# Moving sums, products and bit blocks to other slots in a hash-attention and gated-MLP kernel

## The chip, the cores and the metric

The kernel runs on one core of a Trainium2 chip. The metric is the device time of one execution in microseconds (us). A core has a matrix engine (TensorE, "PE" in the profile; its weight loads are "PEld"), VectorE (DVE), ScalarE (ACT), GpSimd (POOL), and SyncE (SP), which here only issues DMAs. Each engine works through its own list of instructions in order; an instruction that waits holds up everything behind it on that engine.

## The reference

There are 4 batches of 8 heads, 768 tokens and a head size of 64. Each query and key gets a 6-bit bucket from the signs of a projection; attention is allowed only where the buckets agree. The result is 3072 tokens of 512 features, which go through a gated MLP with a residual.

```python
q_bits = (np.einsum('bhsd,dk->bhsk', q, proj) > 0)      # k likewise; 6 bits make a bucket
mask = q_bucket[:, :, :, None] == k_bucket[:, :, None, :]
scores = np.where(mask, scale * q @ k.T, -1e9)
x = softmax(scores) @ v                                  # (3072, 512) after the heads are joined
ffn_out = (gelu(x @ w_gate) * (x @ w_val)) @ w_out       # d_ff = 1536
out = x + sigmoid(x @ w_res) * ffn_out
```

## The kernel before

**Blocks, pairs and slots.** A batch is a block, and has four pairs of heads, so pairs 0 to 15 in all. A pair's scores are made in 9 chunks of 1024 columns (two heads, 71 contracted rows: 64 of the head, 6 bits, one constant). One chunk is a slot, so block b has 36 slots. "Slot 2.5" below is slot 5 of block 2; in the code it is `('a', 2, 5)`. In each slot TensorE computes the scores of its chunk into one of two PSUM tiles `sp` (L500), ScalarE takes the exponential of it (L511), and TensorE multiplies the exponentials of two slots earlier with the values (L475) into an accumulator `av`, one for each head, two buffers.

**Accumulators.** From pair 4 on, an accumulator is opened two slots ahead by a VectorE memset (`opened`, L442), gets a first matmul from TensorE (`preset`, L450), is copied over by VectorE (`repeat`, L454), and when it is full VectorE divides it into the tokens `x_tok` (`finish`, L419 and L420). These slots are fixed by the loop at L606.

**The MLP of the block before** runs in the same slots: `project` (L557 for the residual gate, L571 for the output, one PSUM tile `fps`) hands TensorE two or three matmuls a slot; ScalarE makes `th` (L561), VectorE evicts `fps` with two instructions (L574, L577), SyncE stores.

**Gate and value.** After the 36 slots of a block come twelve steps in `gate_val`, m = 0 to 11; "step g1.9" below is m = 9 of block 1, `('g', 1, 9)` in the code. Each has 8 matmuls for the gate, a gelu by ScalarE into a tile `gt` (L542), 8 matmuls for the value, and a product of the two by VectorE into `hh` (L545). What is listed for a step is issued behind that product. The first step needs the block's tokens turned: a DMA (L428) moves `x_tok` into `x_sb` once the last `finish` of the block is done.

**Bits.** The queries and keys of later pairs get their bits in one of two ways. Pairs 8, 9, 12 and 13 (and 4 to 7 earlier) are transposed by VectorE (L273), hashed on TensorE (L284), and VectorE writes the bits in blocks of four small instructions (`bits`, L305). Pairs 10, 11, 14 and 15 are done without TensorE: for each of the four tensors of two pairs, 12 times, GpSimd multiplies half of the tensor with one column of the projection (`product`, L335, tile `pr`), VectorE sums over the 64 features (`add_up`, L341), and at the end GpSimd compares the sums with zero (`bits_sums`, L344) and SyncE turns the finished rows with a DMA (`turn`, L360). In the text a product and its sum have the same number, 0 to 47 in each block; the products of pair 10 and 11 are block 1's, those of pair 14 and 15 are block 2's. The lists `PLACES`, `LAYS`, `LDY` and `DRAIN` say where each product, each comparison with its turn, each load and the last sums stand.

**What orders the sums.** A product that is put somewhere also puts one sum there, ahead of it, as soon as two products are outstanding; the sum taken is always the oldest product that has none. Products in slots write to the tiles of tag `gt`, shared with gelu's outputs; products in steps write to those of tag `th`, shared with ScalarE's `th`. Each tag has two buffers (L140), so a product waits until the sum of the product two before it in that tag is done. Where the tag changes, the sums left over go to the next block's slot 0, or to the block's slot 35. Block 2's products begin while the last of block 1 are being made, and both use the `gt` buffers in turn.

**Values.** GpSimd also prepares the values of each pair (`vals_s`, `vals_a`, L386 to L398), eight slots ahead of the pair, and casts queries and keys to bf16 (L263, L265).

```python
            if len(left) > 1:
                left.pop(0)
                put(where, b, i, add_up)
            y, n = work[k]
            put(where, b, i, lambda y=y, n=n, tag=tag: product(y, n, tag))
```

Of the kernel before, what the change touches and what calls it, by code (L numbers as in the profile page):

```python
# [80 lines left out]
    (2, 'bits', 4, 0, 'v'), (2, 'turn_dma', 4, 0), (2, 'bits', 4, 1, 'v'), (2, 'turn_dma', 4, 1),  # L81
    (3, 'bits', 5, 0, 'v'), (3, 'turn_dma', 5, 0), (4, 'bits', 5, 1, 'v'), (4, 'turn_dma', 5, 1),
    (1, 'tokens', (6, 7), True), (4, 'cast', 6, 0, 'p'), (5, 'cast', 6, 1, 'p'), (7, 'cast', 7, 0, 'p'),
    (6, 'cast', 7, 1, 'p'), (7, 'bits', 6, 0, 'v'), (7, 'turn_dma', 6, 0), (10, 'bits', 6, 1, 'v'),
    (10, 'turn_dma', 6, 1), (9, 'bits', 7, 0, 'v'), (9, 'turn_dma', 7, 0), (10, 'bits', 7, 1, 'v'),
    (10, 'turn_dma', 7, 1),
]
XDMA = 2
# [4 lines left out]
def kernel(  # L93
# [28 lines left out]


    LDX, TRX, CSX = 9, 26, 26
    LDY = {1: [('a', 1, 0), ('a', 1, 0), ('a', 1, 3), ('a', 1, 1)], 2: [('a', 2, 0), ('a', 2, 2), ('a', 2, 19), ('a', 2, 19)]}
    CSY = [(5, 's'), (5, 's'), (10, 's'), (10, 's')]
    PLACES = {1: [('a', 1, 9), ('a', 1, 10), ('a', 1, 10), ('a', 1, 11), ('a', 1, 13), ('a', 1, 15), ('a', 1, 15), ('a', 1, 16), ('a', 1, 17), ('a', 1, 18), ('a', 1, 18), ('a', 1, 21), ('a', 1, 22), ('a', 1, 23), ('a', 1, 24), ('a', 1, 26), ('a', 1, 27), ('a', 1, 30), ('a', 1, 34), ('g', 1, 0), ('g', 1, 0), ('g', 1, 0), ('g', 1, 1), ('g', 1, 2), ('g', 1, 3), ('g', 1, 3), ('g', 1, 4), ('g', 1, 5), ('g', 1, 5), ('g', 1, 6), ('g', 1, 6), ('g', 1, 7), ('g', 1, 7), ('g', 1, 8), ('g', 1, 8), ('g', 1, 9), ('g', 1, 9), ('g', 1, 10), ('g', 1, 10), ('g', 1, 11), ('a', 2, 2), ('a', 2, 3), ('a', 2, 5), ('a', 2, 6), ('a', 2, 8), ('a', 2, 9), ('a', 2, 13), ('a', 2, 14)], 2: [('a', 2, 1), ('a', 2, 2), ('a', 2, 13), ('a', 2, 14), ('a', 2, 16), ('a', 2, 18), ('a', 2, 19), ('a', 2, 23), ('a', 2, 24), ('a', 2, 24), ('a', 2, 26), ('a', 2, 31), ('a', 2, 32), ('a', 2, 33), ('g', 2, 0), ('g', 2, 0), ('g', 2, 0), ('g', 2, 0), ('g', 2, 1), ('g', 2, 2), ('g', 2, 3), ('g', 2, 3), ('g', 2, 4), ('g', 2, 5), ('g', 2, 5), ('g', 2, 6), ('g', 2, 6), ('g', 2, 7), ('g', 2, 8), ('g', 2, 8), ('g', 2, 9), ('g', 2, 9), ('g', 2, 10), ('g', 2, 10), ('a', 3, 0), ('a', 3, 4), ('a', 3, 4), ('a', 3, 4), ('a', 3, 6), ('a', 3, 7), ('a', 3, 8), ('a', 3, 13), ('a', 3, 13), ('a', 3, 14), ('a', 3, 14), ('a', 3, 15), ('a', 3, 15), ('a', 3, 16)]}
    DRAIN = {1: ('a', 2, 16), 2: ('a', 3, 20)}
    LAYS = {1: [('g', 1, 7), ('g', 1, 8), ('a', 2, 5), ('a', 2, 17)], 2: [('g', 2, 7), ('g', 2, 8), ('a', 3, 6), ('a', 3, 21)]}
    PRS = (1, 8)  # L130
    NE = 9
    C = 2048.0
# [25 lines left out]
    def load(p, side, eng=None):  # L158
        b, hp = divmod(p, HP)
        s = ld_pool.tile([P, HT, D], FP32, tag=f"ld{side}", name=f"ld{side}")  # L160
        (eng or nc.sync).dma_start(
            s.rearrange("p (h t) d -> p h (t d)", h=2),
            (q, k)[side][b, 2 * hp:2 * hp + 2].rearrange("h (p t) d -> p h (t d)", t=T))
        raw[p, side] = s
# [90 lines left out]
    def cast(p, side, eng, c0=0, c1=HT):  # L255
        x = (p, side)
        scale = (1.0 / C) if side == 0 else 1.0
        sl = slice(c0, c1)
        dst = nat_of(x)[:, sl, 0:D]
        if eng is nc.scalar:  # L260
            nc.scalar.activation(dst, raw[x][:, sl], AF.Copy, scale=scale)
        elif side == 0:
            eng.tensor_scalar(dst, raw[x][:, sl], scale, 1.0, op0=ALU.mult, op1=ALU.mult)  # L263
        else:
            eng.tensor_copy(dst, raw[x][:, sl])  # L265
# [325 lines left out]
    def at(s, *pieces):  # L591
        side_work.setdefault(s, []).extend(pieces)
# [4 lines left out]
    def gv(b, m, *pieces):  # L597
        gv_work.setdefault((b, m), []).extend(pieces)
# [23 lines left out]
    def lay(b, m, x):  # L622
        gv(b, m, lambda: bits(*x), lambda: turn(*x))

    def put(where, b, i, *pieces):
        if where == "g":
            gv(b, i, *pieces)
        else:
            at(b * NSLOT + i, *pieces)

    def spread_out(ys, places, drain, lays):
        work = [(y, n) for y in ys for n in range(2 * NBITS)]
        assert len(places) == len(work)
        left, tagged = [], None
        for k, (where, b, i) in enumerate(places):
            tag = "th" if where == "g" else "gt"
            if tagged not in (None, tag):
                for _ in left:
                    put("a", b, 0 if tag == "gt" else NSLOT - 1, add_up)
                left = []  # L640
            tagged = tag
# [5 lines that stand above are left out]
            left.append((y, n))  # L647
        for _ in left:
            put(*drain, add_up)
        for y, p in zip(ys, lays):  # L650
            put(*p, lambda y=y: bits_sums(y), lambda y=y: turn(*y))

    for b in range(B - 1):
# [10 lines left out]
        for m, x in zip((0, 1, 2, 4), xs):  # L664
            lay(b, m, x)
        for y, (where, bb, i) in zip(ys, LDY[b]):
            put(where, bb, i, lambda y=y: load(y[0], y[1]))
        for y, (m, eng) in zip(ys, CSY):
            gv(b, m, lambda y=y, eng=eng: cast(*y, ENG[eng]))
        spread_out(ys, PLACES[b], DRAIN[b], LAYS[b])  # L670
    at(NSLOT + PRS[0], load_rows)
# [31 lines left out]
    def first_gv(i):  # L703
# [8 lines left out]
        cast=lambda p, side, e, *c: cast(p, side, ENG[e], *c),  # L712
# [4 lines left out]
        turn_dma=turn,  # L717
# [14 lines left out]
    for s in range(NSLOT, LAST):  # L732
        p, c = divmod(s, NCH)
# [60 lines left out]
```

## Time and profile before

| | |
|---|---|
| median of three runs | 339.64 us (339.56 to 339.67) |
| the profiled execution | 339.34 us, of which 337.3 us are the span of the trace |
| TensorE busy | 332.4 us of the span |
| VectorE, ScalarE, GpSimd busy | 216.3, 213.8, 175.0 us |
| slots of block 1 | from 78.7 to 120 us of the span |
| slots of block 2 | from 157.4 to 199 us |
| slots of block 3 | from 235.9 to 277 us |

All times within the trace are counted from the span's start. A row of the timeline gives the start, the time until the last of the merged instructions ends, the engine, the line, the operation, the tiles, the shape, the count, and in brackets how long the engine had been idle and what ended that. The recorded ends of matmuls overlap their successors, so waits of TensorE are read from the distance between starts.

### The profile page before, as it was taken

The numbers are of one execution on the slowest core, as the hardware profiler recorded it, in microseconds if no ns is written. First come the engines' busy times: TensorE is split into PE (matmuls) and PEld (weight loads), VectorE is DVE, ScalarE is ACT, GpSimd is POOL, SyncE is SP. The second block draws the span as 40 slices with busy tenths as digits, with TensorE's granted clock in tenths as the row PEclk, the third lists the DMA queues.
The fourth block names the chain that finished last, engine by engine and source line by source line (L and its number), as shares of the span: only waits on it lengthen the run. The fifth ranks groups of instructions, "written<-read, shape, count | busy, mean of one in ns | idle before, by whom it ended". The sixth has DMA issues, their size and how long they took to land.

```text
span 337.3 us, 7740 instructions
## 1 busy us (share of the span) xinstructions
PE 332.4 (99%) x3086; PEld 204.0 (60%) x3086; DVE 216.3 (64%) x458; ACT 213.8 (63%) x247; POOL 175.0 (52%) x260
## 2 busy tenths in 40 slices
PE   8999999999999999999999999999999999999996
PEld 7767665565666655565666665665566665666444
DVE  7977575554577958876577896876577444343243
ACT  4889962337999952437999982255999984322220
POOL 4779920235299943578799972567879100000000
PEclk9999999999999999999999999999999999999999
DMA  7998999999965223518068933825050340000012
GB/s 228 370 289 125 217 242 202 179 166 205 313 222 149 72 85 81 109 32 187 3 167 229 273 92 94 134 47 96 1 126 33 80 101 33 31 2 0 31 64 94
DMA packets 74387, 43.88 MB, mean 130 GB/s; under 512 B 52544, under 2 KB 71360, under 8 KB 74352
## 3 DMA queue, kind: packets, MB, share of 16 engines
q1 hardware_dynamic: 67872, 37.95, 45.3%
q0 software_dynamic: 6400, 5.44, 10.7%
q8 instruction: 24, 0.39, 0.5%
q14 instruction: 11, 0.09, 0.1%
q10 hardware_dynamic: 80, 0.00, 0.0%
HBM read 29.56 MB, written 6.29 MB: 106 GB/s over the span
## 4 chain that ended last, share of the span: by engine, by line
PE 83%; POOL 8%; ACT 4%; DVE 3%; issue 1%; DMA 1%; POOLq 0%; DVEq 0%; ACTq 0%
PE sp L525 37%; PE fps L571 14%; PE sp L500 14%; PE av L475 7%; PE rps L557 5%; POOL pr L335 4%; PE hs L284 3%; ACT ering L511 3%; ACT e L511 1%; PE wps L229 1%; PE pt L373 1%; POOL v L394 1%; DMA x_sb<-x_tok 1%; DVE sums L341 1%; POOL va L386 1%
## 5 line engine op out<-in xcount | busy, mean ns | idle before, releaser
L511 ACT ACTIVATE e<-sp 128x1024 bf16<-128x1024 f32 x117 | 117.7, 1027 | 8.6 <-PE sp L500 3.7
L335 POOL TENSOR_TENSOR pr<-ld,projr 128x384 f32<-128x384 f32 x96 | 93.8, 998 | 47.0 <-DVE sums L341 31.9
L542 ACT ACTIVATE gt<-sp 128x768 bf16<-128x768 f32 x48 | 38.9, 810 | 83.7 <-PE sp L525 80.0
L500 PE MATMUL sp<-aug,aug 71*128 71x256 bf16 (+1 forms) x384 | 86.0, 325 | 0.5
L571 PE MATMUL fps<-wo,hh 128*128 128x512 bf16 (+2 forms) x312 | 79.6, 362 | 0.0
L545 DVE TENSOR_TENSOR hh<-gt,sp 128x768 bf16<-128x768 bf16 x48 | 45.8, 954 | 42.9 <-PE sp L525 39.5
L525 PE MATMUL sp<-x_sb,wg 128*128 128x512 bf16 (+1 forms) x384 | 70.9, 326 | 0.0
L525 PE MATMUL sp<-x_sb,wv 128*128 128x512 bf16 (+1 forms) x384 | 70.9, 326 | 0.0
L475 PEld LDWEIGHTS <-e 128*128 128x128 bf16 x936 | 43.5, 97 | 25.9
L341 DVE TENSOR_REDUCE sums<-pr 128x6 f32<-128x384 f32 x96 | 50.2, 542 | 10.8 <-POOL pr L335 10.3
L525 PEld LDWEIGHTS <-wg 128*128 128x128 bf16 x384 | 37.1, 98 | 25.8 <-issue 1.5
L525 PEld LDWEIGHTS <-wv 128*128 128x128 bf16 x384 | 37.5, 98 | 24.9 <-issue 0.2
L475 PE MATMUL av<-va,e 128*128 128x65 bf16 x936 | 47.0, 193 | 0.0
L571 PEld LDWEIGHTS <-hh 128*128 128x128 bf16 x312 | 28.1, 97 | 21.6
L500 PEld LDWEIGHTS <-aug 71*128 71x128 bf16 x384 | 29.2, 97 | 11.6 <-issue 2.7
L574 DVE SCALAR_TENSOR_TENSOR fps<-th,fps 128x512 f32<-128x512 f32 (+2 forms) x26 | 17.0, 653 | 25.9 <-PE fps L571 25.8
L557 PE MATMUL rps<-wr,x_sb 128*128 128x512 bf16 x96 | 27.1, 379 | 0.0
L511 ACT ACTIVATE ering<-sp 128x1024 bf16<-128x1024 f32 x27 | 25.8, 1031 | 1.7 <-PE sp L500 1.4
L561 ACT ACTIVATE th<-rps 128x512 f32<-128x512 f32 x24 | 14.3, 594 | 18.7 <-PE rps L557 17.5
L273 DVE STREAM_TRANSPOSE t<-ld 128x768 f32<-128x768 f32 (+3 forms) x28 | 23.1, 843 | 1.7 <-DMA ld<-in_q_dram 1.0
L454 DVE COPY av<-av 128x390 f32<-128x390 f32 x24 | 13.6, 565 | 14.6 <-PE av L450 14.5
L263 POOL TENSOR_SCALAR nat<-ld 128x768 bf16<-128x768 f32 (+1 forms) x12 | 9.6, 804 | 19.3 <-DMA aug<-nat 17.4
(76 smaller groups left out, 257.4 us busy)
## 6 DMA issues: line engine op xcount, KB each, us to landing
ldv<-in_v_dram SPq DMA_DIRECT2D x16, 384.0 KB, 5.8
out_dram<-o SPq DMA_DIRECT2D x23, 256.0 KB, 2.3
ld<-in_q_dram SPq DMA_DIRECT2D x15, 384.0 KB, 5.6
ld<-in_k_dram SPq DMA_DIRECT2D x15, 384.0 KB, 5.8
wg<-in_moe_w_gate_dram POOLq DMA_DIRECT2D x4, 384.0 KB, 9.9
wv<-in_moe_w_val_dram POOLq DMA_DIRECT2D x4, 384.0 KB, 10.7
wo<-in_moe_w_out_dram POOLq DMA_DIRECT2D x3, 512.0 KB, 7.6
wr<-in_moe_w_res_dram POOLq DMA_DIRECT2D x1, 512.0 KB, 16.6
```

The lines of the kernel that those rows point to most:

```text
L273: nc.vector.transpose(t32[p, side][:, sl].rearrange("p c h n -> p (c h n)"), raw[p, side][:, sl].rearrange("p c d -> p (c d)"))
L335: nc.gpsimd.tensor_mul(pr, raw[x][:, hi * T:(hi + 1) * T], projr[:, bit].unsqueeze(1).to_broadcast([P, T, D]))
L341: nc.vector.reduce_sum(sums[x][:, hi * T:(hi + 1) * T, bit], pr, axis=mybir.AxisListType.X)
L475: nc.tensor.matmul(av[p, hi][:, qt, :], e[:, off:off + P], va[:, hi, jt, 0:D + 1], start=first, stop=(repeats(p, hi) and jt == T - 1), ski ...
L500: nc.tensor.matmul(sp[:, off:off + nq * P], ks[0:KA, hi * T + jt, :], qs[0:KA, hi * T + qt0:hi * T + qt0 + nq, :], start=True, stop=True)
L511: nc.scalar.activation(e, sp, AF.Exp, scale=float(ALPHA))
L525: nc.tensor.matmul(sp[:, c0:c1], w[:, kk, bass.ts(m, P)], xs[:, kk, c0:c1], start=(kk == 0), stop=(kk == KM - 1))
L542: nc.scalar.activation(gt, sp[:, 0:S], AF.Gelu)
L545: nc.vector.tensor_mul(hidden[b][:, m, :], gt, ps[1][:, 0:S])
L557: nc.tensor.matmul(rps, x_sb[b][:, kk, t, :], wr[:, kk, :], start=(kk == 0), stop=(kk == KM - 1))
L571: nc.tensor.matmul(fps[:, cs], hh[:, m, bass.ts(t, P)], wo[:, m, cs], start=(m == 0), stop=(m == KF - 1))
L574: nc.vector.scalar_tensor_tensor(fps[:, cs], th[:, cs], 1.0, fps[:, cs], op0=ALU.add, op1=ALU.mult)
```

## The change

Nothing is added and nothing is taken away: the same instructions are issued, some of them at other places of their engine's list.

- Block 0, steps: two blocks of bits (four VectorE instructions each) stand one step earlier, pair 7's queries at g0.8 and pair 6's keys at g0.9. Their turns stay.
- Block 1, loads: two loads of pair 11 stand in slot 1.2, one of pair 14 in slot 2.3.
- Block 1, slots 9 to 18 and 29: products 1 and 2 stand in slot 1.9, one slot earlier; products 5 and 17 one slot earlier; products 6 and 7 one slot later; the sums go with them.
- Block 1, steps 9 to 11, and block 2's first slots: products 35 to 39 leave the steps and stand in slot 2.0, with the sums of 33 to 37; they now use the `gt` buffers. Products 40 to 47 stand up to two slots earlier. Two comparisons with their turns (pair 10) stand at g1.8 and g1.11, that of pair 11's keys one slot later.
- Block 2's products: two in block 2 one slot earlier; comparisons of pair 14's queries one step later; in block 3 products 34, 35 and 38, 41 and 45 to 47 one or two slots up or down, the last two sums one slot earlier, two comparisons one slot up or down.

Because `opened`, `repeat` and `finish` stay in their slots, a moved sum can now stand on the other side of one of these memsets or copies on VectorE.

```diff
-    (6, 'cast', 7, 1, 'p'), (7, 'bits', 6, 0, 'v'), (7, 'turn_dma', 6, 0), (10, 'bits', 6, 1, 'v'),
-    (10, 'turn_dma', 6, 1), (9, 'bits', 7, 0, 'v'), (9, 'turn_dma', 7, 0), (10, 'bits', 7, 1, 'v'),
+    (6, 'cast', 7, 1, 'p'), (7, 'bits', 6, 0, 'v'), (7, 'turn_dma', 6, 0), (9, 'bits', 6, 1, 'v'),
+    (10, 'turn_dma', 6, 1), (8, 'bits', 7, 0, 'v'), (9, 'turn_dma', 7, 0), (10, 'bits', 7, 1, 'v'),
...
-    LDY = {1: [('a', 1, 0), ('a', 1, 0), ('a', 1, 3), ('a', 1, 1)], 2: [('a', 2, 0), ('a', 2, 2), ('a', 2, 19), ('a', 2, 19)]}
+    LDY = {1: [('a', 1, 0), ('a', 1, 0), ('a', 1, 2), ('a', 1, 2)], 2: [('a', 2, 0), ('a', 2, 3), ('a', 2, 19), ('a', 2, 19)]}
...
     PLACES = {1:
-      ('a', 1, 9), ('a', 1, 10), ('a', 1, 10), ('a', 1, 11), ('a', 1, 13), ('a', 1, 15), ('a', 1, 15), ('a', 1, 16), ('a', 1, 17),
+      ('a', 1, 9), ('a', 1, 9), ('a', 1, 9), ('a', 1, 11), ('a', 1, 13), ('a', 1, 14), ('a', 1, 16), ('a', 1, 17), ('a', 1, 17),
...
-      ('a', 1, 30), ('a', 1, 34),
+      ('a', 1, 29), ('a', 1, 34),
...
-      ('g', 1, 9), ('g', 1, 9), ('g', 1, 10), ('g', 1, 10), ('g', 1, 11), ('a', 2, 2), ('a', 2, 3),
-      ('a', 2, 5), ('a', 2, 6), ('a', 2, 8), ('a', 2, 9), ('a', 2, 13), ('a', 2, 14)
+      ('a', 2, 0), ('a', 2, 0), ('a', 2, 0), ('a', 2, 0), ('a', 2, 0), ('a', 2, 1), ('a', 2, 2),
+      ('a', 2, 3), ('a', 2, 5), ('a', 2, 8), ('a', 2, 8), ('a', 2, 11), ('a', 2, 13)
     2:
-      ('a', 2, 13), ('a', 2, 14)  ...  ('a', 2, 26), ('a', 2, 31)
+      ('a', 2, 12), ('a', 2, 14)  ...  ('a', 2, 25), ('a', 2, 31)
...
-      ('a', 3, 0), ('a', 3, 4), ('a', 3, 4), ('a', 3, 4), ('a', 3, 6), ('a', 3, 7), ('a', 3, 8),
-      ('a', 3, 13), ('a', 3, 13), ('a', 3, 14), ('a', 3, 14), ('a', 3, 15), ('a', 3, 15), ('a', 3, 16)
+      ('a', 3, 1), ('a', 3, 3), ('a', 3, 4), ('a', 3, 4), ('a', 3, 5), ('a', 3, 7), ('a', 3, 8),
+      ('a', 3, 12), ('a', 3, 13), ('a', 3, 14), ('a', 3, 14), ('a', 3, 17), ('a', 3, 17), ('a', 3, 18)
-    DRAIN = {1: ('a', 2, 16), 2: ('a', 3, 20)}
-    LAYS = {1: [('g', 1, 7), ('g', 1, 8), ('a', 2, 5), ('a', 2, 17)], 2: [('g', 2, 7), ('g', 2, 8), ('a', 3, 6), ('a', 3, 21)]}
+    DRAIN = {1: ('a', 2, 17), 2: ('a', 3, 19)}
+    LAYS = {1: [('g', 1, 8), ('g', 1, 11), ('a', 2, 5), ('a', 2, 18)], 2: [('g', 2, 8), ('g', 2, 8), ('a', 3, 7), ('a', 3, 20)]}
```

More of the change, by code (lines that the diff above doesn't have):

```diff
@@ L124 @@
     LDX, TRX, CSX = 9, 26, 26
-    LDY = {1: [('a', 1, 0), ('a', 1, 0), ('a', 1, 3), ('a', 1, 1)], 2: [('a', 2, 0), ('a', 2, 2), ('a', 2, 19), ('a', 2, 19)]}
+    LDY = {1: [('a', 1, 0), ('a', 1, 0), ('a', 1, 2), ('a', 1, 2)], 2: [('a', 2, 0), ('a', 2, 3), ('a', 2, 19), ('a', 2, 19)]}
     CSY = [(5, 's'), (5, 's'), (10, 's'), (10, 's')]
-    PLACES = {1: [('a', 1, 9), ('a', 1, 10), ('a', 1, 10), ('a', 1, 11), ('a', 1, 13), ('a', 1, 15), ('a', 1, 15), ('a', 1, 16), ('a', 1, 17), ('a', 1, 18), ('a', 1, 18), ('a', 1, 21), ('a', 1, 22), ('a', 1, 23), ('a', 1, 24), ('a', 1, 26), ('a', 1, 27), ('a', 1, 30), ('a', 1, 34), ('g', 1, 0), ('g', 1, 0), ('g', 1, 0), ('g', 1, 1), ('g', 1, 2), ('g', 1, 3), ('g', 1, 3), ('g', 1, 4), ('g', 1, 5), ('g', 1, 5), ('g', 1, 6), ('g', 1, 6), ('g', 1, 7), ('g', 1, 7), ('g', 1, 8), ('g', 1, 8), ('g', 1, 9), ('g', 1, 9), ('g', 1, 10), ('g', 1, 10), ('g', 1, 11), ('a', 2, 2), ('a', 2, 3), ('a', 2, 5), ('a', 2, 6), ('a', 2, 8), ('a', 2, 9), ('a', 2, 13), ('a', 2, 14)], 2: [('a', 2, 1), ('a', 2, 2), ('a', 2, 13), ('a', 2, 14), ('a', 2, 16), ('a', 2, 18), ('a', 2, 19), ('a', 2, 23), ('a', 2, 24), ('a', 2, 24), ('a', 2, 26), ('a', 2, 31), ('a', 2, 32), ('a', 2, 33), ('g', 2, 0), ('g', 2, 0), ('g', 2, 0), ('g', 2, 0), ('g', 2, 1), ('g', 2, 2), ('g', 2, 3), ('g', 2, 3), ('g', 2, 4), ('g', 2, 5), ('g', 2, 5), ('g', 2, 6), ('g', 2, 6), ('g', 2, 7), ('g', 2, 8), ('g', 2, 8), ('g', 2, 9), ('g', 2, 9), ('g', 2, 10), ('g', 2, 10), ('a', 3, 0), ('a', 3, 4), ('a', 3, 4), ('a', 3, 4), ('a', 3, 6), ('a', 3, 7), ('a', 3, 8), ('a', 3, 13), ('a', 3, 13), ('a', 3, 14), ('a', 3, 14), ('a', 3, 15), ('a', 3, 15), ('a', 3, 16)]}
@@ L128 @@
-    DRAIN = {1: ('a', 2, 16), 2: ('a', 3, 20)}
-    LAYS = {1: [('g', 1, 7), ('g', 1, 8), ('a', 2, 5), ('a', 2, 17)], 2: [('g', 2, 7), ('g', 2, 8), ('a', 3, 6), ('a', 3, 21)]}
+    PLACES = {1: [('a', 1, 9), ('a', 1, 9), ('a', 1, 9), ('a', 1, 11), ('a', 1, 13), ('a', 1, 14), ('a', 1, 16), ('a', 1, 17), ('a', 1, 17), ('a', 1, 18), ('a', 1, 18), ('a', 1, 21), ('a', 1, 22), ('a', 1, 23), ('a', 1, 24), ('a', 1, 26), ('a', 1, 27), ('a', 1, 29), ('a', 1, 34), ('g', 1, 0), ('g', 1, 0), ('g', 1, 0), ('g', 1, 1), ('g', 1, 2), ('g', 1, 3), ('g', 1, 3), ('g', 1, 4), ('g', 1, 5), ('g', 1, 5), ('g', 1, 6), ('g', 1, 6), ('g', 1, 7), ('g', 1, 7), ('g', 1, 8), ('g', 1, 8), ('a', 2, 0), ('a', 2, 0), ('a', 2, 0), ('a', 2, 0), ('a', 2, 0), ('a', 2, 1), ('a', 2, 2), ('a', 2, 3), ('a', 2, 5), ('a', 2, 8), ('a', 2, 8), ('a', 2, 11), ('a', 2, 13)], 2: [('a', 2, 1), ('a', 2, 2), ('a', 2, 12), ('a', 2, 14), ('a', 2, 16), ('a', 2, 18), ('a', 2, 19), ('a', 2, 23), ('a', 2, 24), ('a', 2, 24), ('a', 2, 25), ('a', 2, 31), ('a', 2, 32), ('a', 2, 33), ('g', 2, 0), ('g', 2, 0), ('g', 2, 0), ('g', 2, 0), ('g', 2, 1), ('g', 2, 2), ('g', 2, 3), ('g', 2, 3), ('g', 2, 4), ('g', 2, 5), ('g', 2, 5), ('g', 2, 6), ('g', 2, 6), ('g', 2, 7), ('g', 2, 8), ('g', 2, 8), ('g', 2, 9), ('g', 2, 9), ('g', 2, 10), ('g', 2, 10), ('a', 3, 1), ('a', 3, 3), ('a', 3, 4), ('a', 3, 4), ('a', 3, 5), ('a', 3, 7), ('a', 3, 8), ('a', 3, 12), ('a', 3, 13), ('a', 3, 14), ('a', 3, 14), ('a', 3, 17), ('a', 3, 17), ('a', 3, 18)]}
```

## The prediction

> **What bounds the kernel now.** I read the page first, then the chain of waits, then the timeline of TensorE beside those of the engines that release it.
>
> ```profile
> span 337.3 us, 7740 instructions
> PE 332.4 (99%) x3086; PEld 204.0 (60%) x3086; DVE 216.3 (64%) x458; ACT 213.8 (63%) x247; POOL 175.0 (52%) x260
> PE 83%; POOL 8%; ACT 4%; DVE 3%; issue 1%; DMA 1%; POOLq 0%; DVEq 0%; ACTq 0%
> ```
>
> ```profile
> 123.78 2.73 DMA x_sb<-x_tok
> 314.15 2.59 PE fps L571 x12
> ```
>
> TensorE is the bound: busy for 99% and 83% of the chain. Twelve full matmuls follow each other in 2.59 us, so one takes 0.216, and a greater distance between two starts is a wait. Going along TensorE's starts this way I find six waits of 0.05 or more after 78 us. One, behind a gelu of ScalarE in block 3, is not touched; the change can win no more than the sum of the other five. The 8% of POOL in the chain are spells in which TensorE was released just in time; they tell where TensorE would be caught if GpSimd were later.
>
> **The change, place by place.** No instruction is added or dropped, so each part costs only by order. The durations are one profiled execution's, 339.34 us (337.3 of span and 2.04 around it), 0.30 under the median of 339.64; I take the gain off the median unscaled.
>
> *Place 1, the bits at g0.8 and g0.9.*
>
> ```profile
> 77.34 2.01 DVE L305 TENSOR_SCALAR nat<-htp 32x72 bf16<-32x72 f32 x8
> 79.38 0.95 DVE L545 TENSOR_TENSOR hh<-gt,sp 128x768 bf16<-128x768 bf16 x1
> 79.98 0.38 PE L571 MATMUL fps<-wo,hh 128*128 128x512 bf16 x1
> 80.39 0.59 PE L500 MATMUL sp<-aug,aug 71*128 71x256 bf16 x3
> ```
>
> TensorE could go on at 79.98 + 0.216 = 80.20 and went on at 80.39, when the last gate product had freed its `sp`: 0.19 lost. That product stood behind eight bit instructions in 2.01 us. Four of them now stand two steps back, where VectorE is idle, so they cost nothing; the queue before the last product ends 1.0 earlier, and the product starts when its inputs are there, some 0.4 earlier, and ends about 79.9. Gain 0.19. What is late next is TensorE's own work. SyncE's turns wait for the same bits and get no later.
>
> *Place 2, products 1 to 8 of block 1.*
>
> ```profile
> 93.07 0.99 POOL L335 TENSOR_TENSOR pr<-ld,projr 128x384 f32<-128x384 f32 x1 [3.62 <-DVE sums L341]
> 96.89 7.71 POOL L335 TENSOR_TENSOR pr<-ld,projr 128x384 f32<-128x384 f32 x8
> 108.45 0.55 DVE L341 TENSOR_REDUCE sums<-pr 128x6 f32<-128x384 f32 x1 [1.71 <-POOL pr L335]
> 110.17 0.11 DVE L442 MEMSET av<- 128x65 f32 x1
> 109.86 0.60 PE L500 MATMUL sp<-aug,aug 71*128 71x512 bf16 x2
> 110.34 0.20 PE L450 MATMUL av<-vsum,eps_sb 128*128 128x65 bf16 x1
> ```
>
> The accumulator's memset at 110.17 stands behind a sum that waited 1.71 for its product; TensorE's `preset` came at 110.34, where 109.86 + 0.216 + 0.216 leaves 110.29: 0.05 lost. GpSimd had waited 3.62 for the first sum. That sum now stands one slot earlier, so GpSimd resumes about 2 us earlier; the next sums give back some of that (6 and 7 stand a slot later), and I carry 1 us. The memset then comes at about 109.1. Gain 0.05. At the other end, if nothing of the lead survives, it is 0.
>
> *Place 3, the turn of block 1's tokens (product 17 at 1.29).*
>
> ```profile
> 121.18 0.55 DVE L341 TENSOR_REDUCE sums<-pr 128x6 f32<-128x384 f32 x1 [0.39 <-POOL pr L335]
> 121.65 0.69 DVE L574 SCALAR_TENSOR_TENSOR fps<-th,fps 128x512 f32<-128x512 f32 x1
> 123.20 0.56 DVE L420 TENSOR_TENSOR x_tok<-av,rec 128x384 bf16<-128x384 f32 x1
> 123.76 2.75 PE L571 MATMUL fps<-wo,hh 128*128 128x512 bf16 x12
> 126.56 0.48 PE L525 MATMUL sp<-x_sb,wg 128*128 128x512 bf16 x2
> ```
>
> TensorE was done with the twelve matmuls at 123.76 + 2.59 = 126.35 and got the turned tokens at 126.56: 0.21 lost. The chain behind it is the last product, the last sum (121.18), two evictions, `finish`, and a DMA of 2.73. Of the 1 us of lead some 0.8 reaches the last sum. TensorE itself comes 0.24 earlier by places 1 and 2, so 0.45 of lead is enough. Gain 0.21, between 0 and 0.21. Moving product 17 in front of a transpose costs nothing: GpSimd's list there keeps its total.
>
> *Place 4, products 35 to 39 in slot 2.0.*
>
> ```profile
> 157.62 0.95 DVE L545 TENSOR_TENSOR hh<-gt,sp 128x768 bf16<-128x768 bf16 x1 [0.72 <-PE sp L525]
> 158.49 1.01 DVE L341 TENSOR_REDUCE sums<-pr 128x6 f32<-128x384 f32 x2
> 159.59 0.60 ACT L561 ACTIVATE th<-rps 128x512 f32<-128x512 f32 x1 [0.20 <-DVE sums L341]
> 160.09 3.89 ACT L511 ACTIVATE e<-sp 128x1024 bf16<-128x1024 f32 x4
> 160.60 0.41 PE L475 MATMUL av<-va,e 128*128 128x65 bf16 x8
> 161.16 0.59 PE L500 MATMUL sp<-aug,aug 71*128 71x512 bf16 x2
> 163.81 0.19 PE L450 MATMUL av<-vsum,eps_sb 128*128 128x65 bf16 x1
> ```
>
> ScalarE's `th` shares its tile with the products of the steps and waited until 159.50 for sum 38. The next exponential followed it, and TensorE waited for that at 161.16 (eight small matmuls from 160.60 end about 160.85): 0.31 lost. With the change the last product in that tag is 34, so `th` waits for sum 33, the first behind 157.62: 0.46 earlier. The wait goes, 0.31 won at this spot.
>
> It comes back in two ways. First, products 37 to 39 now need sums that come only behind the last gate product: 33, 34, 35 end at 158.49 + 1.01 + 0.46 = 159.96, product 37 starts at 160.03, 39 ends two spacings of 7.71/8 = 0.96 and one duration of 0.99 later at 162.94, its sum at 163.56, and only then comes the memset of slot 2.3, done at 163.69. `preset` follows at 163.74, against 163.81 before. Won there is 0.07, not 0.31. Second, GpSimd is full to the end of the block:
>
> ```profile
> 159.12 1.96 POOL L335 TENSOR_TENSOR pr<-ld,projr 128x384 f32<-128x384 f32 x2 [0.65 <-DMA ld<-in_q_dram]
> 165.15 1.00 POOL L335 TENSOR_TENSOR pr<-ld,projr 128x384 f32<-128x384 f32 x1 [0.25 <-DVE sums L341]
> 168.10 1.95 POOL L335 TENSOR_TENSOR pr<-ld,projr 128x384 f32<-128x384 f32 x2 [1.95 <-DVE sums L341]
> 172.00 1.95 POOL L335 TENSOR_TENSOR pr<-ld,projr 128x384 f32<-128x384 f32 x2 [0.56 <-DVE sums L341]
> 173.91 1.00 POOL L394 TENSOR_TENSOR v<-ldv 128x384 f32<-128x384 f32 x1
> 176.78 4.82 POOL L335 TENSOR_TENSOR pr<-ld,projr 128x384 f32<-128x384 f32 x5
> ```
>
> ```profile
> 172.00:199.63 27.63, 27.63 (x322) 17.31 (x320) 22.15 (x47) 25.41 (x28) 27.10 (x39) 1.00 0.87 230
> ```
>
> ```profile
> 202.27 1.21 SPq L428 DMA_TRANSPOSE x_sb<-x_tok  x1
> 205.08 0.38 PE L525 MATMUL sp<-x_sb,wg 128*128 128x512 bf16 x1
> ```
>
> From 172.00 GpSimd is busy 27.10 of 27.63 (the fifth engine's figure in this row of the windows), up to the last product, whose sum holds the turn of block 2's tokens: issued at 202.27, landed 2.73 later at 205.00, used at 205.08. There is no slack. Between 159.12 and the values at 173.91 GpSimd idled 0.25 + 1.95 + 0.56 = 2.76. Now it starts this stretch 0.91 later (160.03) with two products more (1.92), 2.83 in all, against at most 2.76 of idle time to be filled. Walking its new list I find every sum just done in time, so the idle time is filled and the values come 0.07 later. The turn lands at 205.07, TensorE goes on about 205.11. The whole stage from 157 to 205 then brings -0.03, not +0.31. Bounds: +0.31 if GpSimd should be 0.3 earlier than I count, -2.8 if its idle time stays.
>
> The moved comparisons delay turns that have time: pair 11's first is some 1.5 later, and SyncE's store and loads behind it too, which are needed several slots on. Loads moved by a slot cost nothing for the same reason.
>
> *Place 5, block 3.*
>
> ```profile
> 256.39 0.56 DVE L341 TENSOR_REDUCE sums<-pr 128x6 f32<-128x384 f32 x1 [0.20 <-POOL pr L335]
> 256.96 0.11 DVE L442 MEMSET av<- 128x65 f32 x1
> 256.58 0.60 PE L500 MATMUL sp<-aug,aug 71*128 71x512 bf16 x2
> 257.13 0.20 PE L450 MATMUL av<-vsum,eps_sb 128*128 128x65 bf16 x1
> ```
>
> `preset` at 257.13 could have come at 256.58 + 0.43 = 257.01: 0.12 lost, because the memset of slot 3.16 stood behind the sums of slot 3.15. Those now stand in 3.17, behind it. Gain 0.12. They still run long before their turn is needed, and GpSimd has room there. Products moved in 2.25 and 2.12 keep GpSimd's total: 0.
>
> **Sum.** 0.19 + 0.05 + 0.21 - 0.03 + 0.12 = 0.54. From 339.64 that is **339.10 us** (338.80 for the profiled execution).
>
> **The rivals.**
>
> A, forecast: places 1, 2, 3 and 5 win, place 4 is given back by 205. 339.10, own range 338.95 to 339.25. Chance 0.44.
>
> B, GpSimd's stretch in block 2 is a little shorter than I count (0.3 of 40 us is enough), the stage keeps its 0.31 and all five waits go: 0.88, so 338.76. For it: the count rests on small gaps. Against it: 205.00 to 205.08. Chance 0.30.
>
> C, the lead of GpSimd in block 1 is eaten before the last sum; places 2 and 3 stay: 0.54 - 0.26 = 0.28, so 339.36. Chance 0.08.
>
> D, slower: GpSimd keeps half of its old idle time in block 2, because a sum it needs stands in VectorE behind a `finish` or an eviction. Then it ends 1.4 later instead of 0.07, and with no slack at 205 that goes straight into TensorE's wait: 0.54 - 1.35 = -0.81, so 340.45. It turns to slower than before once 0.54 of that idle time stays. For it: all old idle time there was ended by sums. Chance 0.12.
>
> E, every wait is followed by one as long: 339.6. Chance 0.04.
>
> F, slower: products and sums of the packed stretch run in turn and not side by side. Each of the five products then takes 0.99 + 0.55 = 1.54 instead of 0.96, 2.9 in all, and with no slack at 205: 0.54 - 2.9 = -2.36, so 342.0. Against it: the row at 176.78 has five products in 4.82, with sums of the same tag between them. Chance 0.02. The Trainium skill, page "SBUF — State Buffer", section "SBUF: two separate sides", says that a GpSimd instruction and certain VectorE ones (those with two SBUF inputs, or in a two-port mode) lock a port pair against each other for a whole instruction; a sum that counted among these would make F. By the trace's row it does not count among them.
>
> **How the numbers follow.** The bound of 0.2% (about what a measurement can tell) is 0.68 us: faster below 338.96, slower above 340.32. B is faster (0.30, and 0.02 of A), D and F are slower, the rest within: 0.32, 0.54, 0.14. The range holds A, B, C and E: 338.70 to 339.65.
>
> **What would show it.** In the changed profile: slot 1.1's scores start about 0.2 earlier; no gap before `preset` near 110; the first matmul on `x_sb` near 126.1 follows the twelfth of its row by 0.216; `th` near 159 waits for no sum; `preset` near 163 waits for a memset that stands behind a sum; GpSimd's gaps of 1.95 and 0.56 are gone; TensorE waits for `x_sb` near 205 by some tenths less what came before; no wait near 256. Wrong it would be if GpSimd had gaps between 165 and 199, if the memset of slot 2.3 came earlier than 163.2 in this count, or if a transfer moved by the turns came late.

## The result and the profile after

The changed kernel takes 339.08 us (median of 13 runs, 338.50 to 339.27), the kernel before, beside it, 339.65 (13 runs, 339.27 to 339.99). The medians differ by 0.57 us, and the forecast was 0.54. The ratio on record, 0.9979, is not the ratio of the medians (that is 0.9983): it stands for 0.71 us less, and its 95% interval, 0.9971 to 0.9988, for 0.41 to 0.98 us less.

The profiled execution took 339.27 us. Its page has the answers to the three lines shown of before:

```profile
span 337.2 us, 7740 instructions
PE 332.7 (99%) x3086; PEld 205.2 (61%) x3086; DVE 216.4 (64%) x458; ACT 213.8 (63%) x247; POOL 175.0 (52%) x260
PE 93%; ACT 3%; DVE 1%; POOL 1%; issue 1%; DVEq 0%; ACTq 0%
```

The span is only 0.1 shorter, though the median fell by 0.57. This execution was 0.64 us late before the first instruction that the change touches (the last section has the rows). Two spans can therefore not be compared directly here; what can be compared is the distance between two points of one trace. The chain shows where the work went: GpSimd's 8% are 1% now, and TensorE's 83% are 93%.

The timeline of the changed kernel (start, time until the end, engine, line, tiles, count) at places 1, 2, 3 and 5:

```profile
77.98 1.04 DVE L305 TENSOR_SCALAR nat<-htp 32x72 bf16<-32x72 f32 x4
79.59 0.95 DVE L545 TENSOR_TENSOR hh<-gt,sp 128x768 bf16<-128x768 bf16 x1 [0.58 <-PE sp L525]
80.62 0.38 PE L571 MATMUL fps<-wo,hh 128*128 128x512 bf16 x1
80.84 0.60 PE L500 MATMUL sp<-aug,aug 71*128 71x256 bf16 x3
...
109.75 0.11 DVE L442 MEMSET av<- 128x65 f32 x1
110.32 0.60 PE L500 MATMUL sp<-aug,aug 71*128 71x512 bf16 x2
110.75 0.19 PE L450 MATMUL av<-vsum,eps_sb 128*128 128x65 bf16 x1
...
124.16 2.75 PE L571 MATMUL fps<-wo,hh 128*128 128x512 bf16 x12
126.75 0.49 PE L525 MATMUL sp<-x_sb,wg 128*128 128x512 bf16 x2
...
255.59 0.11 DVE L442 MEMSET av<- 128x65 f32 x1
256.67 0.60 PE L500 MATMUL sp<-aug,aug 71*128 71x512 bf16 x2
257.10 0.19 PE L450 MATMUL av<-vsum,eps_sb 128*128 128x65 bf16 x1
```

Four bit instructions instead of eight stand ahead of the last gate product, and the scores follow the matmul at 80.62 by 0.22, one matmul's time. Both memsets are done well ahead of their `preset` (109.75 for 110.75, 255.59 for 257.10), and each `preset` follows its scores by 0.43, two matmuls. The turned tokens are used at 126.75 = 124.16 + 2.59. All four waits are gone.

Place 4, the same view, and below it two rows of the chain:

```profile
159.49 0.59 ACT L561 ACTIVATE th<-rps 128x512 f32<-128x512 f32 x1
160.79 0.41 PE L475 MATMUL av<-va,e 128*128 128x65 bf16 x8
161.04 0.59 PE L500 MATMUL sp<-aug,aug 71*128 71x512 bf16 x2
163.17 0.55 DVE L341 TENSOR_REDUCE sums<-pr 128x6 f32<-128x384 f32 x1 [0.40 <-POOL pr L335]
163.74 0.11 DVE L442 MEMSET av<- 128x65 f32 x1
163.26 0.60 PE L500 MATMUL sp<-aug,aug 71*128 71x512 bf16 x3
163.91 0.19 PE L450 MATMUL av<-vsum,eps_sb 128*128 128x65 bf16 x1
...
160.23 4.82 POOL L335 TENSOR_TENSOR pr<-ld,projr 128x384 f32<-128x384 f32 x5 [0.39 <-DVE sums L341]
165.01 1.00 POOL L394 TENSOR_TENSOR v<-ldv 128x384 f32<-128x384 f32 x1
167.88 3.87 POOL L335 TENSOR_TENSOR pr<-ld,projr 128x384 f32<-128x384 f32 x4
172.13 1.96 POOL L335 TENSOR_TENSOR pr<-ld,projr 128x384 f32<-128x384 f32 x2
174.05 1.00 POOL L394 TENSOR_TENSOR v<-ldv 128x384 f32<-128x384 f32 x1
202.36 1.21 SPq L428 DMA_TRANSPOSE x_sb<-x_tok  x1
205.17 0.49 PE L525 MATMUL sp<-x_sb,wg 128*128 128x512 bf16 x2
```

```profile
202.74 2.59 PE fps L571 x12
205.33 0.65 PE sp L525 x4
```

`th` carries no bracket: it waits for no sum, and the scores at 161.04 follow the eight small matmuls at once. In exchange `preset` at 163.91 waits for the memset at 163.74, which stands behind the sum at 163.17. GpSimd's rows behind the one at 160.23 carry no bracket either, so the idle times of before are filled. The chain goes from TensorE's twelve matmuls straight to the matmuls on `x_sb` (202.74 + 2.59 = 205.33, in the chain's own times): TensorE does not wait for the turn.

**Where the time went, point by point.** This table gives how much later each point comes than in the trace of before (minus: earlier), read from ScalarE's rows: the exponentials (L511) of the slots named, and the first gelu (L542) that needs a turned block ("turn 1", "turn 2"). A step from one column to the next is what was won or lost between them. The first six columns stand at 82.0, 84.2, 111.8, 127.1, 160.1 and 165.2 us of before. All kernels of the study are in it, each with the one trace that was kept of it (two of the changed kernel, whose steps agree within 0.02); the experiments below go by it.

| kernel | slot 1.2 | 1.4 | 1.28 | turn 1 | 2.1 | 2.6 | 2.31 | turn 2 | 3.2 | 3.19 | 1.2 to 3.19 |
|---|---|---|---|---|---|---|---|---|---|---|---|
| changed | +0.64 | +0.45 | +0.40 | +0.19 | -0.12 | +0.09 | +0.09 | +0.09 | +0.09 | -0.03 | -0.67 |
| changed, second profile | -0.04 | -0.23 | -0.28 | -0.49 | -0.81 | -0.59 | -0.59 | -0.59 | -0.59 | -0.72 | -0.68 |
| no4 | +0.53 | +0.34 | +0.28 | +0.08 | +0.08 | +0.07 | +0.07 | +0.07 | +0.08 | -0.05 | -0.58 |
| only4 | -0.32 | -0.32 | -0.33 | -0.31 | -0.63 | -0.41 | -0.42 | -0.41 | -0.41 | -0.43 | -0.11 |
| open_early | +0.29 | +0.10 | +0.05 | -0.16 | -0.48 | -0.46 | -0.46 | -0.32 | -0.32 | -0.45 | -0.74 |
| only39 | -0.11 | -0.30 | -0.35 | -0.56 | -0.88 | -0.86 | -0.52 | -0.27 | -0.27 | -0.40 | -0.29 |
| only39_turns | -0.09 | -0.29 | -0.34 | -0.54 | -0.86 | -0.85 | -0.84 | -0.84 | -0.84 | -0.97 | -0.88 |
| va_twice | +0.55 | +0.36 | +0.31 | +0.11 | -0.21 | +0.00 | +0.43 | +0.82 | +0.82 | +0.69 | +0.14 |
| first_sum | -0.03 | -0.03 | -0.08 | -0.28 | -0.29 | -0.29 | -0.29 | -0.28 | -0.28 | -0.30 | -0.27 |
| bits_and_last | +0.54 | +0.35 | +0.33 | +0.33 | +0.33 | +0.33 | +0.33 | +0.33 | +0.33 | +0.21 | -0.33 |

In the changed kernel the steps are 0.19 for place 1, 0.05 for place 2, 0.21 for place 3, 0.31 won and 0.21 given back at place 4, and 0.12 for place 5.

### The profile page after: what moved, and what is told of

Its sections match the earlier page's. It is cut to its first block, busy times and chain, and to the rows that moved or that the text cites. A ratio compares the mean times of both kernels' runs of the same rounds, so it can differ in the third digit from the quotient of the medians.

```text
span 337.2 us, 7740 instructions
## 1 busy us (share of the span) xinstructions
PE 332.7 (99%) x3086; PEld 205.2 (61%) x3086; DVE 216.4 (64%) x458; ACT 213.8 (63%) x247; POOL 175.0 (52%) x260
## 4 chain that ended last, share of the span: by engine, by line
PE 93%; ACT 3%; DVE 1%; POOL 1%; issue 1%; DVEq 0%; ACTq 0%
PE sp L525 37%; PE fps L571 18%; PE sp L500 16%; PE av L475 9%; PE rps L557 6%; PE hs L284 3%; ACT ering L511 3%; PE wps L229 1%; PE hs L318 1%; POOL pr L335 1%; PE pt L373 1%; ACT e L511 1%; DVE sums L341 1%; PE pt L459 0%; DVE o L577 0%
## 5 line engine op out<-in xcount | busy, mean ns | idle before, releaser
L511 ACT ACTIVATE e<-sp 128x1024 bf16<-128x1024 f32 x117 | 117.7, 1028 | 8.5 <-PE sp L500 3.4
L542 ACT ACTIVATE gt<-sp 128x768 bf16<-128x768 f32 x48 | 38.9, 811 | 83.5 <-PE sp L525 77.9
L511 ACT ACTIVATE ering<-sp 128x1024 bf16<-128x1024 f32 x27 | 25.8, 1031 | 1.7 <-PE sp L500 1.4
```

Source lines behind the costliest of these rows:

```text
L511: nc.scalar.activation(e, sp, AF.Exp, scale=float(ALPHA))
L542: nc.scalar.activation(gt, sp[:, 0:S], AF.Gelu)
```

## The experiments

### Place 4: is it GpSimd's list that gives the time back?

My theory was the prediction's: the wait at `th` is worth 0.31, the new wait at `preset` takes some of it, and behind that GpSimd's full list sets when the turned tokens of block 2 arrive, so that little more can be had there. The rival was that block 2 is TensorE's alone, and GpSimd's list has room.

**no4**, the changed kernel with place 4 undone:

```diff
-  block 1: ('a', 2, 0) x5 for products 35 to 39, 40 to 47 from ('a', 2, 1) to ('a', 2, 13)
+  block 1: ('g', 1, 9), ('g', 1, 9), ('g', 1, 10), ('g', 1, 10), ('g', 1, 11), 40 to 47 as before
```

> The changed kernel without place 4: products 35 to 47, their last sums, comparisons and the load of pair 14 stand as before; places 1, 2, 3 and 5 stay. Theory T: TensorE waits 0.31 near 161 as before and not near 164; x_sb near 205 is in time by the same hundredths as before; the total is 0.58 under before in the distance between the traces from slot 1.0 on (0.20 + 0.05 + 0.21 + 0.12), only 0.09 more than the changed kernel. A rival by which place 4 brings its whole 0.31 expects 0.30 more than the changed kernel, 0.27 under before.

The load, the comparisons and the last sums of that stretch are as in before too, and so is block 2's product in slot 2.13. **only4** is the kernel before with place 4 alone, the same lines the other way round (block 2's product stays in slot 2.13):

```diff
-  block 1: ('g', 1, 9), ('g', 1, 9), ('g', 1, 10), ('g', 1, 10), ('g', 1, 11), 40 to 47 from ('a', 2, 2) to ('a', 2, 14)
+  block 1: ('a', 2, 0) x5 for products 35 to 39, 40 to 47 as changed
```

> The kernel before with place 4 alone. Theory T: TensorE loses the waits of 0.19 near 80, 0.05 near 110, 0.21 near 126 and 0.12 near 257 as before; near 161 no wait, near 164 a wait of 0.21; from slot 2.6 on TensorE is 0.09 ahead of the kernel before, and keeps that or loses up to 0.05 of it near 205. Rival: 0.3 ahead from slot 2.3 to the end.

Measured: no4 took 339.26 (11 runs; before 339.64), ratio 0.9995, interval 0.9981 to 1.0009, so by the times alone no4 can't be told from before; only4 338.90 in its one run. The table is sharper than the times. In no4 nothing is won between turn 1 and 3.2, and the wait near 161 stands as in before, as the timeline shows: eight small matmuls, which take 0.25 in the changed kernel (160.79 to 161.04), and the next scores 0.55 behind their start.

```profile
160.68 0.41 PE L475 MATMUL av<-va,e 128*128 128x65 bf16 x8
161.23 0.59 PE L500 MATMUL sp<-aug,aug 71*128 71x512 bf16 x2
```

In only4 0.32 is won at slot 2.1, 0.22 given back at 2.6, and 0.10 stays to the end. Place 4 is worth 0.10, with or without the other places.

**open_early**, the changed kernel with the memset at 163.74 two slots earlier, so that it no longer stands behind a sum:

```diff
-            at(s - 2, lambda p=p, hi=hi: opened(p, hi))
+            at(s - (4 if (p, hi) == (8, 1) else 2), lambda p=p, hi=hi: opened(p, hi))
```

> The changed kernel with one memset moved: the accumulator of pair 8's second head is opened in slot 2.1 instead of 2.3, ahead of the sums of products 38 and 39. Theory T (GpSimd's full list sets the end of block 2's slots): the wait of 0.21 at preset near 163.9 goes, TensorE runs 0.21 earlier through block 2's slots, and then waits about 0.2 for x_sb near 205, where the changed kernel has 205.10 landed and 205.17 used; from step g2.0 on the distance to the changed kernel is 0.00 to 0.05, and the time is that of the changed kernel, 0.57 under before. Rival R (the memset alone took the gain back): no wait near 205, the 0.21 stays to the end, 0.78 under before.

Measured: 339.08 (12 runs; before 339.64), ratio 0.9984, interval 0.9973 to 0.9995. The timeline:

```profile
161.47 0.11 DVE L442 MEMSET av<- 128x65 f32 x1
162.91 0.60 PE L500 MATMUL sp<-aug,aug 71*128 71x512 bf16 x3
163.35 0.20 PE L450 MATMUL av<-vsum,eps_sb 128*128 128x65 bf16 x1
```

`preset` follows its scores by 0.44, so the wait is gone. But of the 0.21 only 0.07 reaches the end: at turn 2 the offset falls from -0.46 to -0.32. TensorE arrives 0.2 earlier and the turned tokens hardly do. So in the changed kernel the turn had at most about 0.07 of slack.

**va_twice**, the changed kernel with one GpSimd instruction of block 2 repeated, the cast of pair 11's values in slot 2.19; the result is the same:

```diff
-        nc.gpsimd.tensor_copy(va[:, :, :, 0:D], vs)
+        for _ in range(2 if p == 11 else 1):
+            nc.gpsimd.tensor_copy(va[:, :, :, 0:D], vs)
```

> The changed kernel with the cast of pair 11's values on GpSimd (0.82 us, in slot 2.19) done twice, with the same result: 0.82 more in GpSimd's list of block 2. The theory (no slack from that list to the turned tokens near 205): everything up to slot 2.19 as in the changed kernel, the turned tokens 0.8 later, TensorE waits 0.7 to 0.8 for them near 205, and no other new wait above 0.1; 339.85 against 339.08. The rival (block 2 is TensorE's, GpSimd has some slack): no wait near 205 above 0.2, no change.

Measured: 340.00 in its one run (before 339.42). Against the changed kernel's row of the table, 0.82 is lost between 2.6 and turn 2: all of the added cast. That it is lost was expected; where was not. Its timeline:

```profile
186.03 1.71 POOL L387 CAST va<-ldv 128x768 bf16<-128x768 f32 x2
189.34 0.11 DVE L443 MEMSET av<- 128x65 f32 x1
188.65 0.60 PE L501 MATMUL sp<-aug,aug 71*128 71x512 bf16 x2
189.50 0.20 PE L451 MATMUL av<-vsum,eps_sb 128*128 128x65 bf16 x1 [0.25 <-DVE av L443]
205.90 0.48 PE L526 MATMUL sp<-x_sb,wg 128*128 128x512 bf16 x2 [0.17 <-DMA x_sb<-x_tok]
```

(The repeat adds a line, so L386 is L387 here.) 0.43 is lost already at the `preset` at 189.50, 0.85 behind its scores: a memset stands behind a sum there too, and the sum waits for GpSimd. The other 0.39 is lost up to the turn, 0.33 of it at 205.90. The rival falls: block 2 hangs on GpSimd's list, and at two places.

### Can place 4 keep its 0.31?

It is product 39 that pushes `th` onto a late tile: the tag has two buffers, so `th` takes the tile of product 38, and without 39 in that tag it takes the tile of product 37, whose sum is the first behind the last gate product. **only39** is the changed kernel with products 35 to 38 back in the steps, so that GpSimd's list is not made later:

```diff
-  block 1: ('a', 2, 0), ('a', 2, 0), ('a', 2, 0), ('a', 2, 0), ('a', 2, 0)
+  block 1: ('g', 1, 9), ('g', 1, 9), ('g', 1, 10), ('g', 1, 10), ('a', 2, 0)
```

> The changed kernel with products 35 to 38 back in steps g1.9, g1.9, g1.10, g1.10, where GpSimd is idle; only product 39 stays in slot 2.0 with the gt tile. Theory T: th's tile is that of product 37, whose sum is the first behind the last gate product, so th near 159 still waits for no sum; the memset of slot 2.3 stands behind fewer late sums and is done before 161.5, so preset near 163.6 does not wait; GpSimd enters block 2 about 3 us ahead, so x_sb lands well before 205. All of place 4's 0.30 stays: TensorE 0.2 ahead of the changed kernel from slot 2.5 to the end, 0.78 under before by the median. Rival R expects the same up to 205 and no more; a third view, that any product in slot 2.0 costs what it wins, expects the time of the changed kernel.

Measured: 339.40 (12 runs; before 339.64), ratio 0.9995, interval 0.9984 to 1.0007. The expectation failed. 0.32 was won at slot 2.1 and no wait came at 2.6, but then 0.34 was lost up to 2.31 and 0.25 at turn 2, and by its trace it ended worse than no4 (0.29 won, against 0.58). The rows that tell it, from its timeline (SyncE and GpSimd), its DMA view (size, and us from issue to landing) and its chain:

```profile
153.17 6.62 SPq L360 DMA_TRANSPOSE aug<-nat  x2
159.84 0.87 SPq L161 DMA_DIRECT2D ld<-in_q_dram  x1
163.76 1.00 POOL L335 TENSOR_TENSOR pr<-ld,projr 128x384 f32<-128x384 f32 x1 [3.51 <-DVE av L454]
```

```profile
ld<-in_q_dram SPq DMA_DIRECT2D x1, 384.0 KB, 3.8
```

```profile
202.03 2.74 DMA x_sb<-x_tok
```

GpSimd idled 3.51 us before pair 14's first product. The profile names VectorE's copy, which ends at 163.75, but the load that the product needs was issued at 159.84 and landed 3.8 later, at 163.6. Both ends lie close to the product's start, so this trace alone doesn't decide between them; the next run does. In before the same load was issued at 155.21:

```profile
155.21 0.87 SPq L161 DMA_DIRECT2D ld<-in_q_dram  x1
```

SyncE works in order, and the load stood behind the second turn of pair 10, the later of the two in the row at 153.17 (done at 153.17 + 6.62 = 159.79), which the change had moved to g1.11. That turn needs a comparison on GpSimd, and the comparison now stood behind products 35 to 38. The turn of x_sb at 202.03, back in the chain, is what the idle time cost at the end.

**only39_turns** puts the two comparisons with their turns back where before has them, and is otherwise only39:

```diff
-    LAYS = {1: [('g', 1, 8), ('g', 1, 11), ('a', 2, 5), ('a', 2, 18)],
+    LAYS = {1: [('g', 1, 7), ('g', 1, 8), ('a', 2, 5), ('a', 2, 18)],
```

> The changed kernel with products 35 to 38 back in g1.9 and g1.10 (39 alone stays in slot 2.0) and with the two comparisons of pair 10 back where the kernel before has them. The theory (the wait at th is worth 0.31, it is given back only where GpSimd's list gets longer than its room, and the run with 39 alone lost it because pair 14's load stood behind a turn on SyncE): pair 14's first load is issued near 155.2 and landed before 160 again, GpSimd has no idle stretch above 2.5 us in block 2, no wait near 164, 166, 170 and 205; from slot 1.0 to the end 0.85 to 0.90 less than before (the changed kernel: 0.68), time 338.77 and about 0.2 under the changed kernel's. The rival (the load was not the cause; GpSimd's list is caught by the sums however the loads stand): waits near 166, 170 and 205 as in that run, 0.6 in all, and about 339.4.

> The changed kernel once more, beside the run with 39 alone and pair 10's comparisons back. The theory: 339.0 to 339.15, 0.5 to 0.6 under the kernel before and 0.2 over the other one. The rival: below the other one by 0.3.

Measured side by side: only39_turns 338.70 (12 runs, 338.26 to 339.04), the changed kernel (after_again) 338.93 (12 runs, a little under its expected range), before 339.42, also lower than in the first comparison; ratios to before 0.9979 (0.9966 to 0.9991) and 0.9981 (0.9968 to 0.9994). The medians differ by the expected 0.2, but the two intervals overlap; the traces separate them, 0.88 against 0.68 from slot 1.2 to 3.19. Its timeline:

```profile
154.67 0.86 SPq L161 DMA_DIRECT2D ld<-in_q_dram  x1
155.97 4.83 POOL L335 TENSOR_TENSOR pr<-ld,projr 128x384 f32<-128x384 f32 x5 [0.63 <-DVE sums L341]
167.40 1.96 POOL L335 TENSOR_TENSOR pr<-ld,projr 128x384 f32<-128x384 f32 x2 [1.79 <-DVE sums L341]
171.01 1.95 POOL L335 TENSOR_TENSOR pr<-ld,projr 128x384 f32<-128x384 f32 x2 [1.23 <-DVE sums L341]
172.92 1.00 POOL L394 TENSOR_TENSOR v<-ldv 128x384 f32<-128x384 f32 x1
163.20 0.57 DVE L454 COPY av<-av 128x390 f32<-128x390 f32 x1 [2.77 <-PE av L450]
```

The load is early again and GpSimd goes through five products without a stop. The fifth, from 159.8, is pair 14's first product, and it runs 3.4 us ahead of VectorE's copy, which starts at 163.20 here. So the program doesn't make that product wait for the copy, and it was the load that held it in only39. GpSimd's later idle times (1.79 and 1.23) hurt nobody: the values come at 172.92, 0.40 earlier than in the changed kernel when the turn-1 offset is taken off each (172.92 + 0.54 = 173.46, against 174.05 - 0.19 = 173.86). Of place 4's 0.32, 0.30 is kept. Of all the kernels run, this one has the lowest median and the shortest way through its trace.

### The other four places: does each wait go by itself?

**first_sum** is the kernel before with place 2 alone; product 17 stays in slot 1.30:

```diff
-  block 1: ('a', 1, 9), ('a', 1, 10), ('a', 1, 10), ('a', 1, 11), ('a', 1, 13), ('a', 1, 15), ('a', 1, 15), ('a', 1, 16)
+  block 1: ('a', 1, 9), ('a', 1, 9), ('a', 1, 9), ('a', 1, 11), ('a', 1, 13), ('a', 1, 14), ('a', 1, 16), ('a', 1, 17)
```

> The kernel before with the products and sums of places 2 alone (first sum of block 1 a slot earlier, the next as in the changed kernel up to slot 1.18); product 17 stays in slot 1.30, nothing else is moved. The theory: the wait before preset near 110 goes (0.05) and that for the turned tokens near 126.5 goes too (0.21), as GpSimd's lead of some 0.8 us reaches the last sum of the block by itself: 0.26 less from slot 1.0 on. The rival (place 3's gain comes from product 17's move by a slot): 0.05 goes and the wait near 126.5 stays at 0.21 or grows to 0.26.

Measured: 339.02 in its one run, and in the table 0.05 near 110 and 0.20 at turn 1, nothing elsewhere. Its timeline has the twelve matmuls and the use of the turned tokens 2.59 later:

```profile
123.68 2.75 PE L571 MATMUL fps<-wo,hh 128*128 128x512 bf16 x12
126.27 0.49 PE L525 MATMUL sp<-x_sb,wg 128*128 128x512 bf16 x2
```

GpSimd makes the first product behind the first sum at 91.04 here, where before has 93.07: the 2 us that the prediction counted. So places 2 and 3 have one cause, the moves of products 1 to 7 together, and product 17's move is not needed for it. That the first sum's move alone would do, without those of products 5 to 7, was not run.

**bits_and_last** is the kernel before with place 1 and the last three products of place 5:

```diff
-  (10, 'bits', 6, 1, 'v') ... (9, 'bits', 7, 0, 'v') ... block 2: ('a', 3, 15), ('a', 3, 15), ('a', 3, 16)
+  (9, 'bits', 6, 1, 'v') ... (8, 'bits', 7, 0, 'v') ... block 2: ('a', 3, 17), ('a', 3, 17), ('a', 3, 18)
```

> The kernel before with place 1 (the two blocks of bits) and the last three products of place 5 (slots 3.15, 3.15, 3.16 to 3.17, 3.17, 3.18) alone. The theory: each wait goes by itself, 0.20 near 80 and 0.12 near 257; what TensorE gains near 80 is not lost again, since the first sum of block 1, from which GpSimd's list starts, stands behind a tile that TensorE has to finish and so moves with it: the waits near 110 (0.05), 126.5 (0.21) and 161 (0.31) stay at their old sizes; 0.32 less from slot 1.0 to the end. The rival (GpSimd's list in block 1 does not move with TensorE): the waits near 110 and 126.5 grow by 0.20 in all, what was won near 80 is lost there, and 0.12 is left.

Measured: 339.51 in its one run (before 339.29 in one), with a start 0.54 late; in the table 0.19 near 80, 0.02 near 110, nothing from there to 3.2, then 0.12. What place 1 wins is not lost at the waits of places 2, 3 and 4, which were left in: GpSimd's list in block 1 moves with TensorE. The gains add up: 0.33 here, 0.27 in first_sum and 0.11 in only4 make 0.71, against 0.67 and 0.68 in the two traces of the changed kernel. So the moves that no run took up by themselves (loads, comparisons, the other products of blocks 2 and 3) win nothing more that the table shows.

## Why the prediction was right

**Places 1, 2, 3 and 5** came as forecast: 0.19, 0.05, 0.21 and 0.12, measured 0.19, 0.05, 0.21 and 0.12, each by the mechanism named. For place 3 the prediction put the gain down to GpSimd's lead from place 2; first_sum shows that.

**Place 4** was right in its three parts and off in the size of the last. `th`: forecast 0.31, measured 0.31. `preset`: forecast 163.74 in before's time, which leaves 0.07 of the gain; measured 163.91, or 163.72 when the 0.19 by which the stage starts later in this trace are taken off, which leaves 0.09 (0.10 in the table). The turn at 205: a further 0.10 was to be lost there, and nothing was. So the term is +0.10 in place of -0.03, and the sum 0.67 by the trace instead of 0.54.

The step that failed is the count of GpSimd's idle time, "0.25 + 1.95 + 0.56 = 2.76". I added up what the brackets give. A bracket counts from the recorded end of an instruction, but GpSimd starts the next product before that end: behind the row at 160.23, five products of 1.00 each, the values start after 165.01 - 160.23 = 4.78, so a product takes 0.956 from start to start. Each gap therefore holds 0.04 more than its bracket says (168.10 - 165.15 = 2.95, less 0.96, is 1.99 and not 1.95), and the three gaps 0.12 more. With 2.88 of idle time to fill and 2.83 to fill it with, the values come 0.05 earlier and not 0.07 later: 174.05, less the 0.19, is 173.86, against 173.91. Behind them the list ran 0.05 shorter than in before (202.36 - 174.05 = 28.31, against 202.27 - 173.91 = 28.36; why was not tried). Both together bring the turn 0.10 earlier, as much as TensorE came earlier, and that is why it was just in time.

**The rivals.** B, all five waits gone, did not come: 0.21 is lost at `preset`. Its first half, that GpSimd's stretch is a little shorter than counted, was true, by 0.17 where B asked for 0.3, but TensorE was caught at `preset` before it could use it, and open_early, without that wait, was stopped at the turn (0.74). only39_turns is what B would have been, 0.88 by its trace, which is B's figure. D needed GpSimd to idle between 165 and 199, which it did not; only39 shows D's consequence, from another cause: 3.51 of idle time on GpSimd (for a load, not for a sum), and a loss at 205. C is excluded by the row at 126.75. E fails, since 0.67 of the gains stay. F, products and sums in turn, is excluded again: the sum at 163.17 runs inside the five products at 160.23 without lengthening them (0.956 from start to start, not the 1.54 of F). The Trainium skill's page "SBUF — State Buffer", section "SBUF: two separate sides", lets a GpSimd instruction and certain VectorE instructions shut each other out; by these rows a sum, which has one input, is not one of them, as the prediction had it.

That 339.10 came so near to 339.08 is luck in part: the trace's 0.67 is 0.13 above my sum, and the interval of 0.41 to 0.98 us takes in both.

## What to carry to other kernels

When an instruction is moved, follow each in-order queue that it passes: a comparison put behind four GpSimd products held a turn on SyncE, and the load behind the turn, and that cost more than the move was worth (0.59 lost, 0.32 won). Read a packed engine by the distance between starts, not by recorded ends or idle brackets. Where many small waits are tuned, compare two traces point by point from the first instruction that differs; one run's total says little about gains of a tenth of a percent.

## What was not expected of the hardware

The start-up, whose code is the same in every kernel here, differs by up to 0.96 us from run to run (slot 1.2's exponential comes from 0.32 earlier to 0.64 later than in before). Most of it arises before 7 us, in the first matmuls that hash the queries and keys. The timeline of the changed kernel's first profile, and then of before:

```profile
3.91 1.94 PE L318 MATMUL hs<-t,projs 128*128 128x128 f32 x8
5.64 1.14 PE L318 MATMUL wps<-t,projs 128*128 128x128 f32 x4
```

```profile
3.88 1.30 PE L318 MATMUL hs<-t,projs 128*128 128x128 f32 x8
5.02 0.66 PE L318 MATMUL wps<-t,projs 128*128 128x128 f32 x4
```

The same twelve matmuls start 0.03 apart and need 2.87 us in the one and 1.80 in the other, and no wait is recorded. Their single starts show a change of rate: most are 0.21 apart at first and 0.11 apart afterwards. The view of windows gives a granted clock of 1.00 for the whole stretch, but it gives 1.00 also where a trace holds no record of the clock. The trace's record itself begins, with full clock, at 4.35 us in before and at 6.63 in the changed kernel, and that is where the spacing halves (in no4, 5.71 us: the first eight matmuls take 1.69 from 4.09 to 5.78, the four behind them 0.66). Over all eleven traces this point lies between 3.50 us, in only4, which has the earliest slot 1.2, and 6.63, in the changed kernel's first trace, which has the latest. What sets that moment in a run was not tried and stays open.
